# GpSimd turns both heads of the second pair, and the stacking transfers are issued one slot earlier

## The chip, the cores and the metric

The kernel runs on one core of one Trainium2 chip. The metric is the device time of one execution in microseconds (us); lower is better. A core has five engines that run side by side, each through its own instructions in order: TensorE (PE in the rows; its weight loads are PEld), VectorE (DVE), ScalarE (ACT), GpSimd (POOL) and SyncE (SP), which here issues every transfer by DMA. Engines wait for each other and for transfers by semaphores.

## The reference, cut to what matters

Attention with rotary position embedding, and behind it two feed-forward blocks. The change lies in the attention.

```python
B, H, S, D = 4, 8, 576, 64                     # q, k, v
rotate(x) = concat([x1 * cos - x2 * sin, x1 * sin + x2 * cos])   # x1, x2: halves of D
scores = rotate(q) @ rotate(k).T / sqrt(D)
attn = exp(scores - max); attn = attn / (sum(attn) + 1e-9)
x = attn @ v                                   # then as (2304, 512)
x = (sigmoid(x @ w_gate) * (x @ w_val)) @ w_out            # 512 -> 1536 -> 512
h = x @ w_in; solu = h * softmax(h); out = layernorm(solu) * g_ln @ w_out2
```

## The kernel before, in words

The 32 pairs of batch and head are worked on two heads at a time: 16 pairs (`pairs`, numbered 0 to 15 here). A pair has nine tiles of 128 queries, and the main loop goes through 16 x 9 = 144 slots, one tile of queries in each. In a slot TensorE makes the scores (`scores`, tile `s`, line 364), VectorE takes the negative maximum (`row_max`, `nm`, line 371), ScalarE the exponentials with their sums (`exps`, `e`, line 376); TensorE transposes `e` (`te`), and ScalarE and VectorE take it out of PSUM as a high and a low part (`et`, lines 426 and 429, `evac_h` and `evac_l`); TensorE multiplies by v (`av`, line 476). Every matrix product is made of high and low parts, so that operands are kept twice.

Work that belongs to other pairs is woven into the slots by a table, `SLOTS`: a number there is a slot counted from the first slot of the pair that it is for. `at(...)` puts a call into the agenda of a slot, and within a slot calls stand in the order in which they were put there, the lower pair first. For pair i:

- `load_qk` brings q and k (`raw`, lines 208 and 212), `load_v` brings v (`rawv`, lines 220 and 225).
- `turn` rotates q and k of both heads in four steps, two products (line 242) and two sums (line 250), on GpSimd unless it is told another engine. For pair 1 it was called for head 0 on GpSimd and for head 1 on VectorE. Pair 0 is turned by `turn_first` (lines 266 and 250).
- `qk_bank` transposes the result on TensorE (`tq`, lines 298 and 301), and it is taken out of PSUM into the tile `st` (lines 426 and 429), at slots -11, -9 and -8.
- `stack` lets five transfers by SP copy halves of `st` between the partitions (lines 310 to 314), since scores need high and low parts above each other. The fourth and fifth write over what the first three read, so SP stands at line 313 until those have landed. Behind all five come the first `scores` of the pair. Pairs 0 and 1 are stacked by ScalarE and VectorE as well (`stack_first`, lines 323 to 329).
- `split_v` (ACT line 281, POOL line 282) splits v; `stack_left` (line 335) copies the last 64 queries to the tile `qtl`.
- After the pair's scores: `weigh` adds 1e-9 to the sums on GpSimd (line 388) and takes the reciprocal on VectorE (line 389); `weigh_out` stores it to DRAM (`d<-rt`, line 403); `spread` reads it back to all partitions in four transfers (`wt<-d`, line 411); `join` moves one head's output beside the other's (`um<-uw`, line 482), `add` adds the two parts on GpSimd (line 488), and `scale_x` multiplies by the weights on GpSimd (line 421).

SP, GpSimd and VectorE go through this strictly in order, so what a table entry moves is also a place in three queues. In slot 21 of pair i-3 stands its `spread`, which is the slot -6 of pair i.

Of the kernel before, what the change touches and what calls it, by code (L numbers as in the profile page):

```python
# [20 lines left out]
def kernel(  # L21
# [21 lines left out]
    nc = tc.nc  # L43
# [158 lines left out]
    def load_qk(i, t=None):  # L202

        b, hp = pairs[i]
        hs = slice(2 * hp, 2 * hp + 2)
        raws[i] = t = raw_p.tile([P, 2, NSL, D], F32, tag="raw", name=f"raw{i}") if t is None else t
        for j, src in enumerate((k, q)):
            yield nc.sync.dma_start(
                out=t[:, :, 4 * j:4 * j + 4, :], in_=src[b, hs, 0:MAIN, :].rearrange("h (p r) d -> p h r d", r=4)
            )  # L210
        for j, src in enumerate((k, q)):
            yield nc.sync.dma_start(
                out=t[j * LEFT:(j + 1) * LEFT, :, 8, :], in_=src[b, hs, MAIN:S, :].rearrange("h t d -> t h d")
            )

    def load_v(i):
        b, hp = pairs[i]
        hs = slice(2 * hp, 2 * hp + 2)
        t = rawv_p.tile([P, 10, D], F32, tag="rawv", name=f"rawv{i}")
        nc.sync.dma_start(  # L220
            out=t[:, 0:8, :].rearrange("p (h r) d -> p h r d", h=2),
            in_=v[b, hs, 0:MAIN, :].rearrange("h (p r) d -> p h r d", r=4),
        )
        for j in range(2):
            nc.sync.dma_start(
                out=t[j * LEFT:(j + 1) * LEFT, 8:10, :], in_=v[b, hs, MAIN:S, :].rearrange("h t d -> t h d")
            )
        vraws[i] = t
# [3 lines left out]
    def turn(i, step, hs=slice(0, 2), eng=nc.gpsimd):  # L232

        if i not in others:
            others[i] = rot_p.tile([P, 2, NSL, D], F32, tag="other", name=f"other{i}")
        if step == 2 and i not in turned:
            turned[i] = rot_p.tile([P, NSL, 2, D], F32, tag="turned", name=f"turned{i}")
        n = NSL * (hs.stop - hs.start)
        x, o = (t[:, hs].rearrange("p h i (a d) -> p (h i) a d", a=2) for t in (raws[i], others[i]))
        if step < 2:  # L240
            w = rope_sb[:, 1 - step, hs].rearrange("p h i d -> p (h i) d").unsqueeze(2)
            eng.tensor_mul(out=(o, x)[step], in0=x, in1=w.to_broadcast([P, n, 2, D // 2]))
        else:
            turn_end(i, step, eng, hs, slice(0, NSL))

    def turn_end(i, step, eng, hs, sl):
        a = step - 2
        here, there = (slice(c * D // 2, (c + 1) * D // 2) for c in (a, 1 - a))
        op = eng.tensor_sub if a == 0 else eng.tensor_add
        op(  # L250
            out=turned[i][:, sl, hs, here].rearrange("p i h d -> p h i d"),
            in0=raws[i][:, hs, sl, here],
            in1=others[i][:, hs, sl, there],
        )

    def turn_first(table):

        others[0] = rot_p.tile([P, 2, NSL, D], F32, tag="other", name="other0")
        turned[0] = rot_p.tile([P, NSL, 2, D], F32, tag="turned", name="turned0")
        x, o = (t.rearrange("p h i (a d) -> p h i a d", a=2) for t in (raws[0], others[0]))  # L260
        for hs, sl, eng in FIRST_PARTS:
            n = sl.stop - sl.start
            for step in range(2):
                for h in range(hs.start, hs.stop):
                    w = rope_sb[:, 1 - step, h, sl] if sl.start == 4 else table[:, 1 - step, sl if n > 1 else slice(4, 5)]
                    eng.tensor_mul(
                        out=(o, x)[step][:, h, sl], in0=x[:, h, sl],
                        in1=w.unsqueeze(2).to_broadcast([P, n, 2, D // 2]),
                    )
            for step in (2, 3):  # L270
                turn_end(0, step, eng, hs, sl)
# [16 lines left out]
    def qk_bank(i, part):  # L288

        raw = turned[i].rearrange("p i h d -> p i (h d)")  # L290
        if part == 0:
            stacks[i, 0] = qk_p.tile([P, 2, 2, S], F32R, tag="st0", name=f"st0_{i}")
            stacks[i, 1] = qk_p.tile([P, 3, S], F32R, tag="st1", name=f"st1_{i}")
        st = stacks[i, 0]
        ps = ps_t.tile([P, 512], F32, tag="t", name=f"tq{i}_{part}")
        if part < 2:
            for r in range(4):
                nc.tensor.transpose(ps[:, r * P:(r + 1) * P], raw[:, 4 * part + r, :], ident)
            h_out, l_out, src = st[:, 0, part, 0:MAIN], st[:, 1, part, 0:MAIN], ps
        else:  # L300
            nc.tensor.transpose(ps[:, 0:P], raw[:, 8, :], ident)
            h_out, l_out = st[:, 0, :, MAIN:S], st[:, 1, :, MAIN:S]
            src = ps[:, 0:P].rearrange("p (a t) -> p a t", a=2)
        return [(h_out, l_out, src)]
# [215 lines left out]
    FIRST, GROUP, ATTEND, REST = "first", "group", "attend", "rest"  # L520
    agenda = {}

    def at(g, kind, fn, *args):
        agenda.setdefault((g, kind), []).append((fn, args))


    SLOTS = dict(
        te=(1, 3, 4, 5, 6, 7, 8, 9, 11),
        corner=8,
        left=(6, 11),  # L530
        av=(((6, 2), (8, 9)), ((9, 4), (10, 9)), ((11, 2), (12, 6), (13, 9)), ((14, 9),)),
        join=(18, 19),
        add=(20, 24),
        weigh=11,
        weigh_t=13,
# [2 lines left out]
        scale=24,  # L538
        turn=(-16, -16, -15, -15),
        bank=(-11, -9, -8),  # L540
        stack=-6,
        split_v=-1,
        stack_left=0,
        load_qk=-23,
# [6 lines left out]
        bank1=(1, 1, 1),  # L551
        stack1=3,
        first_b=(-1, -1, 2),
        turn1=(0, 0, 0, 0),
        split_v0=0,
        stack_left0=0,
    )
# [60 lines left out]
    def evacuate_h(evs):  # L618
        for ev in evs:
            evac_h(*ev)  # L620
# [58 lines left out]
    if True:  # L679

        spare_1 = et_p.tile([P, 16 * S], F32, tag="et", name="spare1")
        table = spare_1[:, 2 * NSL * D:2 * NSL * D + 2 * 5 * D // 2].rearrange("p (c i d) -> p c i d", c=2, i=5)
        first_loads = load_qk(0)
        next(first_loads)
        nc.sync.dma_start(out=table, in_=rope)
        for _ in first_loads:
            pass
        for h in range(2):
            nc.scalar.activation(out=rope_sb[:, :, h, 4:8], in_=table[:, :, 0:4], func=AF.Copy, scale=D ** -0.5)
        for _ in load_qk(1, spare_1[:, 0:2 * NSL * D].rearrange("p (h i d) -> p h i d", h=2, i=NSL)):  # L690
            pass
        nc.sync.dma_start(out=g_sb, in_=moe2_g_ln.rearrange("(k p) -> p k", p=P))
        load_v(0)
        load_v(1)
        turn_first(table)
        for h in range(2):
            nc.scalar.copy(out=rope_sb[:, :, h, 0:4], in_=table[:, :, 0:4])
            nc.scalar.copy(out=rope_sb[:, :, h, 8:9], in_=table[:, :, 4:5])
        first.extend(qk_bank(0, part)[0][2] for part in range(3))
        for m in range(3):  # L700
            stack_first(0, m)
            at(SLOTS["first_b"][m], REST, stack_first, 1, m)
        at(SLOTS["stack_left0"], REST, stack_left, 0)
        at(SLOTS["split_v0"], REST, split_v, 0)
        for m in range(4):
            turn(1, m, slice(0, 1))
            at(SLOTS["turn1"][m], REST, turn, 1, m, slice(1, 2), nc.vector)
        for fn, args in agenda.pop((-1, REST), []):
            fn(*args)

        sc = scores(0, 0)
        for g in range(NPR * NTL):
            i, n = divmod(g, NTL)
            if g == (NPR - 1) * NTL:
                prep_ctx.close()
                xs_pool["p"] = x_ctx.enter_context(tc.tile_pool(name="xs", bufs=XS, side="right", reuse_waits="tile"))
            if g == 1:
                et = et_p.tile([P, 2, 2, 4, S], F32R, tag="et", name="et")
            nm = row_max(i, n, sc)
            if SLOTS["exp_pos"] == 0:  # L720
                exps(i, n, sc, nm)
            evacuate_h(cur)
            if SLOTS["exp_pos"] == 1:
                exps(i, n, sc, nm)
            evacuate_h(late)
            if SLOTS["exp_pos"] == 2:
                exps(i, n, sc, nm)
            evacuate_u()
            if SLOTS["exp_pos"] == 3:
                exps(i, n, sc, nm)  # L730
            evacuate_l()
            if g + 1 < NPR * NTL:
                sc = scores(*divmod(g + 1, NTL))
            advance(g)
# [381 lines left out]
```

## Time and profile before

| | |
|---|---|
| median of 3 runs | 980.09 us (976.26 to 981.96) |
| the profiled execution, its own time | 977.19 us |
| its span, from first to last instruction | 975.4 us |
| PE, DVE, ACT, POOL busy in the span | 933.8, 651.7, 505.5, 445.6 us |
| transfers issued by SP, share of 16 DMA engines | 34.6% |
| attention, first score to last | 11.5 to 299.3 us |
| granted TensorE clock, mean | 0.998 of full speed |

Busy shares over the whole span mix three stages. The attention ends near 300 us, and only there do the changed lines run; after it comes the first feed-forward block and then the second.

### The profile page before, as it was taken

How to read it: one execution, taken by the hardware profiler on the slowest of the kernel's cores; microseconds unless marked ns; L12 is line 12 of the kernel's file. 1: busy time of each engine (PE TensorE's matmuls, PEld its weight loads, DVE VectorE, ACT ScalarE, POOL GpSimd, SP SyncE). 2: the span in 40 equal slices, each digit the busy share in tenths (PEclk: the TensorE clock that was granted, in tenths of full speed). 3: DMA queues.
4: the chain of work that ended last, by engine and by line, in shares of the span. 5: the costliest groups of instructions: out<-in, count | busy, mean ns of one | idle time of the engine just before them, and what ended most of it. 6: DMA issues, size and time to landing. Idle time of an engine off the chain costs nothing.

```text
span 975.4 us, 14436 instructions
## 1 busy us (share of the span) xinstructions
PE 933.8 (96%) x5128; PEld 798.6 (82%) x5128; DVE 651.7 (67%) x1073; ACT 505.5 (52%) x994; POOL 445.6 (46%) x356
## 2 busy tenths in 40 slices
PE   4999999999999899999999999999999989999998
PEld 3889899898988588898788898788898868888886
DVE  8999989999988945346245365544456787666561
ACT  4889989898986323133111123112123576666662
POOL 5668889889835533334314344324343531121110
PEclk9999999999999999999999999999999999999999
DMA  4666677676654320103101012100111334334231
GB/s 109 142 163 165 156 184 180 162 177 154 166 131 133 90 65 22 44 23 100 30 22 42 24 44 87 44 22 22 44 45 63 109 64 88 66 75 87 65 76 44
DMA packets 92311, 86.10 MB, mean 88 GB/s; under 512 B 52608, under 2 KB 77456, under 8 KB 92240
## 3 DMA queue, kind: packets, MB, share of 16 engines
q1 hardware_dynamic: 92240, 85.19, 34.6%
q8 instruction: 40, 0.66, 0.3%
q14 instruction: 31, 0.25, 0.1%
HBM read 46.83 MB, written 4.79 MB: 53 GB/s over the span
## 4 chain that ended last, share of the span: by engine, by line
PE 63%; DVE 13%; DMA 10%; POOL 6%; issue 4%; SPq 2%; ACT 2%; DVEq 0%; POOLq 0%; ACTq 0%
PE gv L673 9%; PE gv L674 9%; PE gv L672 9%; DMA st<-st 8%; PE y L783 4%; PE y L782 4%; PE y L781 4%; PE po L970 3%; PE po L969 3%; PE po L971 3%; PE ph L874 3%; PE ph L876 3%; PE ph L875 3%; DVE nm L371 2%; DVE val L121 2%
## 5 line engine op out<-in xcount | busy, mean ns | idle before, releaser
L767 POOL TENSOR_TENSOR gs<-g,gs 128x512 fp32r<-128x512 f32 (+1 forms) x59 | 74.1, 1256 | 268.1 <-DVE gs L766 242.0
L762 ACT ACTIVATE sg<-gv 128x512 f32<-128x512 f32 (+1 forms) x60 | 33.3, 556 | 295.9 <-PE gv L674 295.9
L672 PE MATMUL gv<-xs,w 128*128 128x512 f32 (+1 forms) x480 | 178.5, 372 | 2.3 <-ACT w L135 2.3
L674 PE MATMUL gv<-xs,w 128*128 128x512 f32 (+1 forms) x480 | 178.6, 372 | 2.1 <-POOL w L136 1.7
L673 PE MATMUL gv<-xs,w 128*128 128x512 f32 (+1 forms) x480 | 178.6, 372 | 0.3 <-DVE xs L507 0.2
L764 DVE TENSOR_TENSOR g<-gv,sg 128x512 f32<-128x512 f32 (+1 forms) x60 | 38.2, 636 | 181.4 <-ACT sg L762 181.3
L364 PE MATMUL s<-st 128*128 128x288 f32 x512 | 103.1, 320 | 15.3 <-DMA st<-st 8.1
L376 ACT ACTIVATE e<-s,nm 128x576 f32<-128x576 f32 x144 | 107.8, 748 | 19.0 <-DVE nm L371 17.7
L371 DVE TENSOR_REDUCE nm<-s 128x1 f32<-128x576 f32 x144 | 107.3, 746 | 5.5 <-PE s L364 4.0
L674 PEld LDWEIGHTS gv<-xs,w 128*128 128x128 f32 x480 | 90.0, 188 | 20.8 <-POOL w L136 2.8
L672 PEld LDWEIGHTS gv<-xs,w 128*128 128x128 f32 x480 | 90.0, 188 | 20.2 <-ACT w L135 3.2
L673 PEld LDWEIGHTS gv<-xs,w 128*128 128x128 f32 x480 | 90.1, 188 | 18.9 <-DVE xs L507 1.9
L429 DVE TENSOR_TENSOR et<-te,et 128x512 fp32r<-128x512 f32 x144 | 98.7, 687 | 10.1 <-ACT et L426 8.2
L476 PE MATMUL av<-et,vs 128*128 128x288 f32 x512 | 99.5, 315 | 0.7 <-DVE uw L625 0.5
L364 PEld LDWEIGHTS s<-st 128*128 128x128 f32 x512 | 75.3, 193 | 25.3 <-ACT e L376 9.0
L783 PE MATMUL y<-gs,w 128*128 128x512 f32 (+1 forms) x240 | 89.3, 372 | 0.0
L781 PE MATMUL y<-gs,w 128*128 128x512 f32 (+1 forms) x240 | 89.1, 371 | 0.0
L782 PE MATMUL y<-gs,w 128*128 128x512 f32 (+1 forms) x240 | 89.1, 371 | 0.0
L435 PE MATMUL te<-ident,e 128*128 128x128 f32 x576 | 86.4, 273 | 0.3 <-DVE et L429 0.3
L426 ACT CAST et<-te 128x512 fp32r<-128x512 f32 x144 | 84.1, 586 | 3.0 <-PE te L435 2.8
L476 PEld LDWEIGHTS av<-et,vs 128*128 128x128 f32 x512 | 72.9, 189 | 2.2 <-DVE uw L625 1.6
L435 PEld LDWEIGHTS te<-ident,e 128*128 128x128 f32 x576 | 70.8, 141 | 0.7 <-DVE et L429 0.5
(128 smaller groups left out, 1963.8 us busy)
## 6 DMA issues: line engine op xcount, KB each, us to landing
wraw<-in_moe_w_out_dram SPq DMA_DIRECT2D x20, 512.0 KB, 3.9
st<-st SPq DMA_DIRECT2D x30, 288.0 KB, 3.1
st<-st SPq DMA_DIRECT2D x15, 432.0 KB, 4.0
wraw<-in_moe_w_gate_dram SPq DMA_DIRECT2D x12, 512.0 KB, 4.1
wraw<-in_moe_w_val_dram SPq DMA_DIRECT2D x12, 512.0 KB, 4.8
um<-uw SPq DMA_DIRECT2D x32, 144.0 KB, 2.4
st<-st SPq DMA_DIRECT2D x30, 144.0 KB, 4.9
rawv<-in_v_dram SPq DMA_DIRECT2D x16, 256.0 KB
```

Source lines behind the costliest of these rows:

```text
L364: nc.tensor.matmul(ps[:, j, :HALF], w, x, start=m == 0, stop=m == len(mm) - 1)
L371: nc.vector.tensor_reduce(out=nm, in_=ps[:, :, :HALF], axis=AX.XY, op=ALU.max, negate=True)
L376: nc.scalar.activation(out=e.rearrange("p (j c) -> p j c", j=2), in_=ps[:, :, :HALF], func=AF.Exp, bias=nm, accum_out=sums[i][:, sum_at[n] ...
L429: nc.vector.tensor_sub(out=l_out, in0=ps, in1=h_out.bitcast(F32))
L435: nc.tensor.transpose(ps[:, r * P:(r + 1) * P], e[:, r * P:(r + 1) * P], ident)
L476: nc.tensor.matmul(av[:, :HALF], *mm[m], start=m == 0, stop=m == len(mm) - 1)
L672: nc.tensor.matmul(ps[:, :n], wh, x[:, 0, :n], start=kk == 0, stop=False)
L673: nc.tensor.matmul(ps[:, :n], wh, x[:, 1, :n], start=False, stop=False)
L674: nc.tensor.matmul(ps[:, :n], wl, x[:, 0, :n], start=False, stop=kk == KD - 1)
L781: nc.tensor.matmul(ys[m][:, :n], wh, g[:, 0, :n], start=first, stop=False)
L782: nc.tensor.matmul(ys[m][:, :n], wl, g[:, 0, :n], start=False, stop=False)
L783: nc.tensor.matmul(ys[m][:, :n], wh, g[:, 1, :n], start=False, stop=last)
```

## The change

Two things change. The entry `stack` of the table goes from -6 to -7, so that the five stacking transfers of pairs 2 to 15 are put into the agenda one slot earlier. And for pair 1 `turn` is called once for both heads on GpSimd, where it was called for head 0 on GpSimd and for head 1 on VectorE.

```diff
@@ SLOTS
         bank=(-11, -9, -8),
-        stack=-6,
+        stack=-7,
         split_v=-1,
...
-        turn1=(0, 0, 0, 0),
@@ before the main loop
         for m in range(4):
-            turn(1, m, slice(0, 1))
-            at(SLOTS["turn1"][m], REST, turn, 1, m, slice(1, 2), nc.vector)
+            turn(1, m)
```

On SP, the rows from the stacking of pair 4 to that of pair 5 stood like this before (`st_4` and `st_5` are the pairs' tiles, `wt` is the spread of pair 1 and then 2, `raw` the loads of pair 6).

```order
L310 DMA st_4_946<-st_4_945 64x1728
L311 DMA st_4_946<-st_4_945 64x1152
L312 DMA st_4_946<-st_4_945 64x576
L313 DMA st_4_945<-st_4_945 64x1152
L314 DMA st_4_945<-st_4_945 64x576
L208 DMA raw_1141<-in_k_dram 128x2x256
...
L482 DMA um_1290<-uw_0_919 64x576
L482 DMA um_1290<-uw_1_1067 64x576
L220 DMA rawv_1320<-in_v_dram 128x2x256
L225 DMA rawv_1320<-in_v_dram 64x2x64 x2
L411 DMA wt_1384<-d_1175 64x512 x2
L411 DMA wt_1384<-d_1175 64x64 x2
L310 DMA st_5_1224<-st_5_1223 64x1728
```

With the change they stand like this.

```order
L314 DMA st_4_941<-st_4_941 64x576
L411 DMA wt_1108<-d_895 64x512 x2
L411 DMA wt_1108<-d_895 64x64 x2
L208 DMA raw_1137<-in_k_dram 128x2x256
...
L403 DMA d_1171<-rt_1169 9x128
L482 DMA um_1286<-uw_0_915 64x576
L482 DMA um_1286<-uw_1_1063 64x576
L220 DMA rawv_1316<-in_v_dram 128x2x256
L225 DMA rawv_1316<-in_v_dram 64x2x64 x2
L310 DMA st_5_1220<-st_5_1219 64x1728
```

The four `wt` transfers of a spread went from just ahead of a pair's five stacking transfers to just behind them; nothing else changed its place on SP, and the same happens at pairs 4 to 15.

On GpSimd, the start of the program differs in the rows that turn pair 1 (`spare_131` holds its q and k, `turned_206` the result).

```order
-L242 TENSOR_TENSOR other_203<-spare_131,rope_sb 128x576
-L242 TENSOR_TENSOR spare_131<-spare_131,rope_sb 128x576
-L250 TENSOR_TENSOR turned_206<-spare_131,other_203 128x9x32 x2
+L242 TENSOR_TENSOR other_203<-spare_131,rope_sb 128x1152
+L242 TENSOR_TENSOR spare_131<-spare_131,rope_sb 128x1152
+L250 TENSOR_TENSOR turned_206<-spare_131,other_203 128x2x9x32 x2
 L335 CAST qtl_78<-st_0_179 128x64
 L335 CAST qtl_78<-st_0_180 128x64
 L282 TENSOR_TENSOR vs_239<-rawv_145,vs_239 128x10x64
```

The same four instructions are twice as wide, and the copies to `qtl`, the split of v and the turn of pair 2 follow behind them as before. On VectorE, at the same time, four instructions are gone between the maxima of the first two tiles of queries.

```order
 L371 TENSOR_REDUCE nm_0_223<-s_0_217 128x1
-L242 TENSOR_TENSOR other_203<-spare_131,rope_sb 128x576
-L242 TENSOR_TENSOR spare_131<-spare_131,rope_sb 128x576
-L250 TENSOR_TENSOR turned_206<-spare_131,other_203 128x9x32 x2
```

The maximum of the second tile now follows that of the first directly. On TensorE and ScalarE no instruction changes its place.

## Rows read from the trace of the kernel before

**Rows 1.** Busy time by stretch, one pair each: engines, granted clock, DMA share, GB/s.
```profile
103.31:121.60 18.29, 16.80 (x132) 16.11 (x132) 17.20 (x30) 16.88 (x41) 14.63 (x11) 1.00 0.64 154
...
211.29:229.31 18.02, 16.72 (x132) 16.19 (x132) 17.75 (x29) 15.57 (x37) 15.80 (x12) 1.00 0.70 170
```

**Rows 2.** Waits, 60 to 290 us: us in total, times, longest us.
```profile
PE s L364 <- DMA st<-st: 7.8, 15, 1.2
```

**Rows 3.** Timeline of TensorE at the end of pair 5: start, us, what, idle before.
```profile
119.12 0.63 PE L298 MATMUL tq<-ident,turned 128*128 128x128 f32 x4
120.89 0.37 PE L364 MATMUL s<-st 128*128 128x288 f32 x1 [1.14 <-DMA st<-st]
121.60 0.67 PE L364 MATMUL s<-st 128*128 128x288 f32 x3 [0.34 <-DMA st<-st]
```

**Rows 4.** Timeline of SP's issues between the stackings of pairs 5 and 6.
```profile
99.96 0.54 SPq L314 DMA_DIRECT2D st<-st  x1
...
104.14 1.15 SPq L482 DMA_DIRECT2D um<-uw  x2
...
107.39 2.47 SPq L411 DMA_DIRECT2D wt<-d  x4
110.35 0.48 SPq L310 DMA_DIRECT2D st<-st  x1
```

**Rows 5.** Timeline of VectorE at the same place.
```profile
110.04 0.28 DVE L429 TENSOR_TENSOR st<-tq,st 128x128 fp32r<-128x128 f32 x1
110.24 0.21 DVE L389 RECIPROCAL sum<-sum 128x9 f32<-128x9 f32 x1
```

**Rows 6.** Timeline of SP at the stacking of pair 9.
```profile
165.31 0.54 SPq L310 DMA_DIRECT2D st<-st  x1
```

**Rows 7.** Timeline of VectorE at the stacking of pair 9.
```profile
164.44 0.28 DVE L429 TENSOR_TENSOR st<-tq,st 128x128 fp32r<-128x128 f32 x1
```

**Rows 8.** Timeline of GpSimd in pair 5.
```profile
101.19 1.42 POOL L421 TENSOR_TENSOR x_sb<-x_sb,wt 128x576 f32<-128x576 f32 x1
105.01 1.57 POOL L282 TENSOR_TENSOR vs<-rawv,vs 128x640 fp32r<-128x640 f32 x1 [2.40 <-ACT vs L281]
...
106.90 1.45 POOL L488 TENSOR_TENSOR x_sb<-uw,um 64x576 f32<-64x576 f32 x1
108.43 0.25 POOL L388 TENSOR_SCALAR sum<-sum 128x9 f32<-128x9 f32 x1
...
114.28 2.82 POOL L250 TENSOR_TENSOR turned<-raw,other 128x576 f32<-128x576 f32 x2
```

**Rows 9.** Transfers, 60 to 280 us: count, KB each, median us to landing.
```profile
um<-uw SPq DMA_DIRECT2D x24, 144.0 KB, 2.4
...
wt<-d SPq DMA_DIRECT2D x24, 16.0 KB, 2.9
```

**Rows 10.** Timeline of GpSimd at the start.
```profile
10.02 1.40 POOL L242 TENSOR_TENSOR other<-spare,rope_sb 128x576 f32<-128x576 f32 x1 [1.51 <-DVE turned L250]
11.50 1.41 POOL L242 TENSOR_TENSOR spare<-spare,rope_sb 128x576 f32<-128x576 f32 x1
...
22.27 2.64 POOL L242 TENSOR_TENSOR raw<-raw,rope_sb 128x1152 f32<-128x1152 f32 x1
```

**Rows 11.** Timeline of VectorE at the start.
```profile
11.73 1.50 DVE L329 CAST st<-st 64x576 fp32r<-64x576 f32 x1
...
15.66 0.76 DVE L242 TENSOR_TENSOR other<-spare,rope_sb 128x576 f32<-128x576 f32 x1
...
17.25 2.17 DVE L250 TENSOR_TENSOR turned<-spare,other 128x288 f32<-128x288 f32 x2
...
23.08 2.15 DVE L329 CAST st<-st 64x576 fp32r<-64x576 f32 x1
```

**Rows 12.** Timeline of TensorE at the start.
```profile
19.57 1.94 PE L298 MATMUL tq<-ident,turned 128*128 128x128 f32 x8 [1.69 <-DVE turned L250]
...
25.37 0.90 PE L364 MATMUL s<-st,qtl 128*128 128x288 f32 x5 [1.15 <-DVE st L329]
```

## The prediction, made before the changed kernel was run

> **What bounds the kernel now.** I first read the busy time by stretch, cut at the starts of pairs, because the change lies in the attention alone and a share over the whole span says nothing there. The reader sees that TensorE and VectorE are both nearly full: in the stretch of pair 5 TensorE is busy 16.80 us and VectorE 17.20 us of 18.29 us, and in pair 11 VectorE is busy 17.75 us of 18.02 us [rows 1]. So an idle microsecond of VectorE may or may not be covered, depending on the pair. Next I read the waits: TensorE waits 7.8 us in 15 waits for the stacking transfers `st<-st`, all at the first scores of a pair [rows 2]; the worst case is the end of pair 5, where it stands 1.14 us and then 0.34 us, 1.48 us together [rows 3]. That is what an earlier stacking could win. Then I asked what starts the stacking. The transfer of line 310 is issued at 110.35 us. VectorE finishes the last part of `st` at 110.04 + 0.28 = 110.32 us, and SP had finished the spread ahead of it at 107.39 + 2.47 = 109.86 us [rows 4, 5]. The stacking is released by VectorE's data, not by its place in SP's queue.
>
> **The change, part by part. The order on SP.** Between two stackings SP issues the same transfers as before; only the spread goes from their end to their beginning. So SP is free for the next stacking at the same time as before, and the data come when they came: the first scores gain nothing in a pair like that of rows 4. There are pairs in which SP was late: in pair 9 the data are there at 164.44 + 0.28 = 164.72 us and line 310 is issued at 165.31 us, 0.59 us later [rows 6, 7]. There the spread, now early, fills time in which SP waited for `uw` and `rt`, and part of the 0.59 us may come back. I take 0.5 us for the whole run, between 0 and 1.0 us.
>
> **What is now late.** Everything that SP issues between the stackings comes 2.47 us later, and the spread itself much later. GpSimd stands behind both. In pair 5 the stacking's last issue ends at 99.96 + 0.54 = 100.50 us [rows 4]. The spread would be issued from 100.55 us; its last transfer starts some 1.9 us on (three quarters of 2.47) and lands 2.9 us after that [rows 4, 9], at 105.35 us. `scale_x`, which ran at 101.19 us, waits for it, and ends at 105.35 + 1.42 = 106.8 us; `split_v` and the two copies to `qtl` behind it take 106.90 - 105.01 = 1.89 us, to 108.7 us [rows 8]. The other way gives the same: `um` is issued at 104.14 + 2.47 = 106.61 us and lands 2.4 us later, at 109.0 us [rows 4, 9]. So the first `add` begins near 109.05 us, not 106.90 us, 2.15 us late, and the sum of line 388, which ends 108.43 + 0.25 - 106.90 = 1.78 us after the add began, is ready at 110.83 us [rows 8]. VectorE reaches the reciprocal that needs it at 110.24 us [rows 5]. It must stand 0.6 us, and queued behind it are the maximum and the `et` parts of the next tiles, for which ScalarE and TensorE wait. The stacking is not hit: its data are written just ahead of the reciprocal.
>
> **How much of that reaches the end.** Where TensorE waits for the stacking at the end of the pair, 0.6 us of delay disappears in that wait (1.48 us in pair 5). The sum of these waits, 7.8 us over the twelve pairs concerned, is 0.65 us for each, as large as the stall, but uneven: pair 11, with 0.27 us of VectorE's time free, has no cover. I take two pairs of nine or ten that lose their 0.6 us: 1.2 us, between 0 and 9 x 0.6 = 5.4 us.
>
> **The turn.** GpSimd's turn in pair 5 ends at 114.28 + 2.82 = 117.10 us, and `tq` starts at 119.12 us [rows 8, 3]. 2.15 us later it ends at 119.25 us, so `tq` starts up to 0.15 us late. Right behind `tq` stands the wait of 1.48 us that hides it; I take nothing. Without that cover it would be 0.15 us a pair, 1.8 us in twelve.
>
> **Pair 1.** VectorE loses the four instructions from 15.66 us to 17.25 + 2.17 = 19.42 us, and `tq` of pair 1 starts behind them at 19.57 us [rows 11, 12]. GpSimd starts its turn at 10.02 us [rows 10]. At full width a product takes 2.64 us and, as between the two at half width (11.50 - 10.02 - 1.40), 0.08 us pass before the next, 2.72 us from start to start [rows 10]; the two sums take 2.82 us [rows 8]: 10.02 + 2 x 2.72 + 2.82 = 18.3 us, 1.1 us ahead of VectorE's end. The next thing on VectorE is the cast of line 329. In both rows it lasts until 0.32 us after the GpSimd product beside it: 11.73 + 1.50 = 13.23 us against 11.50 + 1.41 = 12.91 us, and 23.08 + 2.15 = 25.23 us against 22.27 + 2.64 = 24.91 us [rows 10, 11]. With the change GpSimd begins pair 2's turn at 18.3 us, plus 1.89 us for the copies and the split [rows 8], plus 0.2 us of gaps: 20.4 us. Its first product ends near 23.1 us, the cast comes near 22.0 us and ends at 23.4 us instead of 25.23 us. TensorE waits for that cast (1.15 us at 25.37 us, [rows 12]), and from there on runs without a long pause. The gain is between 1.1 us (`tq`) and 1.8 us (cast); I take 1.6 us. If the cast is more than 1 us later than I think it falls into the second product and ends after 23.1 + 2.72 + 0.32 = 26.1 us, 0.9 us late. So the bounds are a gain of 1.8 us and a loss of 0.9 us. Pair 2's turn then ends near 20.4 + 2 x 2.72 + 2.82 = 28.7 us, and its transposes are called only in slot 7 of pair 0.
>
> A product that VectorE did in 0.76 us takes GpSimd 1.40 us at the same size [rows 10, 11], a factor of 1.84, so the move makes work; it gains only because GpSimd begins 5.6 us earlier. The Trainium skill (GPSIMD Engine Reference, "Engine selection") speaks against such a move: two-input elementwise work is about twice as slow on GpSimd. An estimate by that factor gives a product of both heads 4 x 0.76 = 3.04 us and, with the sums as long as a product, an end at 10.02 + 3 x 3.04 = 19.1 us; the gain at `tq` would be 0.3 us, not 1.1 us. The rows have the durations themselves, so they decide.
>
> **The sum.** -0.5 - 1.6 + 1.2 = -0.9 us on the profiled execution's 977.19 us (span 975.4 us and 1.8 us around it), which gives 976.3 us. That execution lies 2.9 us below the median of the runs, 980.09 us; on the median it is 979.2 us. What a measurement here can tell from no change is about 0.5%, 4.9 us.
>
> **The rivals.** *The stacking lands earlier* (faster). If freeing the transfers from the spread ahead of them, in SP's queue or in the DMA engines, ended TensorE's waits, all 7.8 us would go: 980.1 - 7.8 - 1.6 = 970.7 us. For it speaks that the spread is issued 0.5 us ahead of line 310; against it, that line 310 waited for VectorE until 110.32 us. *The late sum stops VectorE in every pair* (slower). The place is the reciprocal; it decides from the point where the sum comes more than a pair's cover late, 1.48 us in pair 5 and less elsewhere. If the spread or `um` landed 1 us later than before, nine stalls of 1.6 us less the cover of 7.8 us leave 6.6 us, together with the other terms +4.5 us: 984.6 us. For it speaks that both ways into the add are late at once; against it, that 0.6 us is within most covers. *The first cast loses to GpSimd* (little change). With wide products the cast that came at 11.73 us could wait for the second one, to 10.02 + 2 x 2.72 + 0.2 = 15.7 us instead of 13.23 us. VectorE's next pieces shift by 2.4 us, the third scores end near 20.3 us, and `tq` behind them is 0.7 us later than before instead of earlier: +0.7 - 0.5 + 1.2 = +1.4 us, 981.5 us. Against it: in both rows the cast got in after one product. The Trainium skill (SBUF — State Buffer, "Who interferes with whom") has the rule behind this rival: a cast of VectorE in a two-port mode and a GpSimd instruction exclude each other for the whole instruction, and the one that issues first goes first. The 0.32 us in both rows agree with it; who goes first beside wider products no row shows.
>
> **How the numbers follow.** My forecast 0.62, the earlier stacking 0.10, the stop in every pair 0.16, the lost cast 0.12. The range takes the bounds of the terms (-2.8 us at best without the rival, +7.2 us at worst) with the median's own spread in three runs, and reaches half way to the first rival: 973.5 to 985.0 us. Faster by over 0.5%: the first rival and little else, 0.14. Slower by over 0.5%: the worse half of the second and a tail, 0.13. Within 0.5%: 0.73.
>
> **What would show it.** Right: line 310 still starts within 0.1 us of VectorE's last part of `st`; `scale_x` and the first add wait for `wt` and `um`; the reciprocal is preceded by an idle 0.5 to 0.7 us that ends with GpSimd's sum; TensorE's waits for `st<-st` shrink by about what VectorE lost; pair 1's `tq` starts near 18.4 us and the second cast ends near 23.4 us. Wrong: pairs that last over 0.5 us longer with the wait at the reciprocal over 1 us, or pairs of 17.1 us without waits for `st<-st`.

## The result, and the profile of the changed kernel

The changed kernel takes 987.95 us (median of 6 runs, 985.64 to 992.3), the kernel before on the same chip 975.92 us (6 runs, 974.93 to 981.96). The ratio is 1.0108, with a 95% interval from 1.0085 to 1.013: slower by 1.1%, above my range. The profiled execution took 985.64 us, its span is 983.9 us.

Of the two parts of the change, the turn of pair 1 came as worked out. The timelines of GpSimd, VectorE and TensorE at the start answer to [rows 10 to 12]:

```profile
10.05 2.62 POOL L242 TENSOR_TENSOR other<-spare,rope_sb 128x1152 f32<-128x1152 f32 x1 [1.51 <-DVE turned L250]
...
15.57 2.77 POOL L250 TENSOR_TENSOR turned<-spare,other 128x576 f32<-128x576 f32 x2
...
20.18 2.67 POOL L242 TENSOR_TENSOR other<-raw,rope_sb 128x1152 f32<-128x1152 f32 x1
```

```profile
11.75 1.24 DVE L329 CAST st<-st 64x576 fp32r<-64x576 f32 x1
...
21.94 1.22 DVE L329 CAST st<-st 64x576 fp32r<-64x576 f32 x1
```

```profile
18.40 1.97 PE L298 MATMUL tq<-ident,turned 128*128 128x128 f32 x8 [0.77 <-POOL turned L250]
...
23.31 0.91 PE L364 MATMUL s<-st,qtl 128*128 128x288 f32 x5 [0.48 <-DVE st L329]
```

GpSimd's turn ends at 18.34 us, `tq` starts at 18.40 us (I said 18.4), and the second cast ends at 23.16 us (I said 23.4). Pair 5 starts at 101.20 us, not 103.31 us [rows 1]: 2.1 us gained, where I had taken 1.6 us.

All of that and more is then lost. I cut the attention from the second score product of pair 4 to that of pair 15, eleven pairs. Three views of busy time by stretch follow (columns as in [rows 1]): the eleven pairs of the changed kernel, those of the kernel before, and pairs 5 and 11 of the changed kernel.

```profile
84.10:290.10 206.00, 187.94 (x1437) 176.90 (x1437) 187.59 (x306) 176.04 (x413) 158.81 (x120) 1.00 0.65 158
```

```profile
86.20:281.80 195.60, 185.71 (x1437) 176.99 (x1437) 182.07 (x306) 176.20 (x412) 160.03 (x120) 1.00 0.69 165
```

```profile
101.20:119.86 18.66, 17.26 (x132) 16.13 (x131) 17.33 (x30) 17.14 (x42) 14.65 (x12) 1.00 0.64 153
...
213.90:235.53 21.63, 17.28 (x131) 16.26 (x132) 19.14 (x29) 15.45 (x37) 17.14 (x13) 1.00 0.62 156
```

Eleven pairs last 10.4 us longer. VectorE is busy 5.52 us longer with the same number of instructions (x306), so some of its instructions have become slower; and pair 11 alone lost 3.61 us (21.63 against 18.02 us), 1.39 us of it in VectorE's busy time. The clock was full in both, so it isn't that. The waits from 60 to 290 us, first of the changed kernel, then of the kernel before (the stacking's is in [rows 2]):

```profile
ACT e L376 <- DVE nm L371: 19.8, 23, 2.1
...
PE s L364 <- ACT e L376: 9.9, 12, 1.7
...
DVE sum L389 <- POOL sum L388: 7.1, 7, 2.4
POOL x_sb L488 <- DMA um<-uw: 6.1, 6, 2.2
...
PE s L364 <- DMA st<-st: 4.1, 8, 1.2
```

```profile
ACT e L376 <- DVE nm L371: 8.1, 18, 1.5
...
PE s L364 <- ACT e L376: 1.7, 3, 0.7
...
DVE sum L389 <- POOL sum L388: 1.1, 1, 1.1
```

VectorE waits 7.1 us at the reciprocal (before 1.1 us, once), and TensorE now waits 9.9 us for exponentials that stand behind VectorE (before 1.7 us), while its wait for the stacking fell from 7.8 to 4.1 us. What stood there, in pair 11, on GpSimd, SP and VectorE:

```profile
217.51 1.57 POOL L282 TENSOR_TENSOR vs<-rawv,vs 128x640 fp32r<-128x640 f32 x1
...
221.32 1.44 POOL L488 TENSOR_TENSOR x_sb<-uw,um 64x576 f32<-64x576 f32 x1 [1.89 <-DMA um<-uw]
222.85 0.25 POOL L388 TENSOR_SCALAR sum<-sum 128x9 f32<-128x9 f32 x1
...
225.89 2.65 POOL L242 TENSOR_TENSOR raw<-raw,rope_sb 128x1152 f32<-128x1152 f32 x1
```

```profile
211.19 2.81 SPq L411 DMA_DIRECT2D wt<-d  x4
...
217.49 1.15 SPq L482 DMA_DIRECT2D um<-uw  x2
```

```profile
220.64 0.28 DVE L429 TENSOR_TENSOR st<-tq,st 128x128 fp32r<-128x128 f32 x1
223.13 0.21 DVE L389 RECIPROCAL sum<-sum 128x9 f32<-128x9 f32 x1 [2.22 <-POOL sum L388]
...
226.72 2.38 DVE L121 SCALAR_TENSOR_TENSOR val<-mag,val 128x512 int32<-128x512 int32 x1
```

The reader sees two things. First, `um` is issued behind the moved spread, the add starts 3.83 us after that issue, and VectorE stands 2.22 us for the sum. GpSimd stood idle for the last 1.89 us of that, so `um` itself took long as well. The profile tells the landing of only a few `um` transfers: in the changed kernel from 60 to 290 us, and in the kernel before from 60 to 280 us:

```profile
DMA to landing us min/median/max: 2.4/2.7/4.5
```

```profile
DMA to landing us min/median/max: 2.3/2.4/4.6
```

A landing as slow as that was there before the change as well. In the DMA records of 215 to 224 us two packets of instructions lie beside the data (`um` is 144 KB; the columns are packets, MB, share of 16 engines):

```profile
q8 instruction: 1, 0.02, 1.1%
q14 instruction: 1, 0.01, 0.5%
```

That such a packet made `um` late is argued from the time, not shown: the slowest landing of the first view, of a transfer issued at 198.10 us, has no packet of instructions beside it, but a 512 KB weight load issued just ahead of it (197.43 us). Second, line 121 takes 2.38 us. It is one of VectorE's shifts with two inputs in SBUF that decode feed-forward weights, woven into pairs 7, 9 and 11, and it ends (229.10 us) 0.56 us after GpSimd's product of line 242 (228.54 us), which began 0.83 us ahead of it. All three executions of each of the two shifting lines, in the view of one source line, changed kernel first:

```profile
L121 DVE SCALAR_TENSOR_TENSOR val<-mag,val x3: 2375/2404/2412, 149.9 to 226.7; 128x512 int32<-128x512 int32 x3
...
L124 DVE SCALAR_TENSOR_TENSOR val<-wraw,val x3: 681/1714/1723, 155.0 to 231.8; 128x512 int32<-128x512 int32 x3
```

```profile
L121 DVE SCALAR_TENSOR_TENSOR val<-mag,val x3: 679/1042/1819, 150.5 to 221.8; 128x512 int32<-128x512 int32 x3
...
L124 DVE SCALAR_TENSOR_TENSOR val<-wraw,val x3: 681/681/1740, 153.9 to 225.6; 128x512 int32<-128x512 int32 x3
```

Line 121 grows by 7.19 - 3.54 = 3.65 us and line 124 by 4.12 - 3.10 = 1.02 us: 4.7 us of the 5.52 us. The Trainium skill (SBUF — State Buffer, "Who interferes with whom") says that a VectorE instruction with two SBUF inputs and a GpSimd instruction that reads SBUF exclude each other, whichever issues first. The rows agree: the shift ends 0.56 us after the product, and alone it takes 0.68 us.

### The profile page after: what moved, and what is told of

Same layout as the page of the kernel before. It is cut to its first block, busy times and chain, and to the rows that moved or that the text cites. A ratio compares the mean times of both kernels' runs of the same rounds, so it can differ in the third digit from the quotient of the medians.

```text
span 983.9 us, 14406 instructions
## 1 busy us (share of the span) xinstructions
PE 936.5 (95%) x5128; PEld 799.7 (81%) x5128; DVE 652.0 (66%) x1069; ACT 505.5 (51%) x994; POOL 447.8 (46%) x356
## 4 chain that ended last, share of the span: by engine, by line
PE 63%; DVE 14%; DMA 10%; issue 4%; POOL 4%; SPq 2%; ACT 2%; POOLq 0%; DVEq 0%; ACTq 0%
PE gv L672 9%; PE gv L673 9%; PE gv L671 9%; DMA st<-st 8%; PE y L781 4%; PE y L779 4%; PE y L780 4%; PE po L968 3%; PE po L967 3%; PE po L969 3%; PE ph L872 3%; PE ph L873 3%; PE ph L874 3%; DVE nm L371 3%; DVE et L429 2%
```

## The experiments

**Theories.** A: the late spread makes GpSimd late, by `um` and `wt`, and VectorE waits at the reciprocal. B (rival): GpSimd's new timing puts its products over VectorE's shifts. C (rival): the stacking's new place on SP is itself the harm. Ratios are to the kernel before on the same chip. "Eleven pairs" is the stretch from the second score of pair 4 to that of pair 15 in the profiled execution: before 195.6, changed 206.0 us. It is one execution of each kernel, so it can differ from the medians by some us.

**The two halves of the change.**

```diff
 e1_stack_only, on the kernel before:   -stack=-6  +stack=-7
 e2_turn_only, on the changed kernel:   -stack=-7  +stack=-6
```

> The table entry of the stacking at -7, pair 1 turned by both engines as before. If the loss is all the spread's new place on SP (theory A), the gain at the start is missing and the loss stays: the pairs from 5 on lose the 10.4 us that the changed kernel's trace shows, 985 to 990 us, ratio to before 1.010 to 1.014. If the loss came with the turn on GpSimd (theory B), this one is as fast as before, 975 to 978 us.

> Pair 1 turned on GpSimd alone, the stacking at -6 as before. Theory A: about 2 us faster than before (first scores of pair 4 near 84.1 us instead of 86.2 us), 973 to 975 us, ratio 0.997 to 0.9985, and the pairs behind keep their length. Theory B: slower than before by most of the 10 us.

Stacking alone: 1.0118 (1.0102 to 1.0133); turn alone: 0.9968 (0.9955 to 0.998), 974.75 us against 978.06 us. The whole loss is the table entry, and the turn alone gains 2.0 to 4.4 us, as the 2.1 us of the trace; its eleven pairs take 195.6 us. Line 121 took 1.67 to 2.41 us in the first and 0.68 to 1.79 us in the second.

**The sum on VectorE.** This takes the reciprocal away from GpSimd's queue.

```diff
-        sum_eng=0,
+        sum_eng=1,
```

> The changed kernel with the 1e-9 added to the sums by VectorE, so that its reciprocal no longer waits for GpSimd. If the wait at the reciprocal (7.1 us in 7 pairs) is the whole loss, the time comes down to that of the turn alone, 973 to 976 us. If VectorE's weight decoding under GpSimd's turn is the larger part, only some 3 to 5 us come back: 982 to 985 us, and line 121 still takes about 2.4 us in its three pairs.

1.0142 (1.0128 to 1.0156), eleven pairs 209.9 us: slower still, a miss. The wait is gone, and line 121 took only 0.87 to 1.15 us in pairs 7, 9 and 11, but the addition of nine numbers a partition now runs on VectorE beside GpSimd's product. One such place, on VectorE and on GpSimd:

```profile
92.98 2.77 DVE L388 TENSOR_SCALAR sum<-sum 128x9 f32<-128x9 f32 x1
95.78 0.21 DVE L389 RECIPROCAL sum<-sum 128x9 f32<-128x9 f32 x1
```

```profile
93.05 2.66 POOL L242 TENSOR_TENSOR other<-raw,rope_sb 128x1152 f32<-128x1152 f32 x1
```

It ends at 95.75 us, 0.04 us after the product, though it is recorded 0.07 us ahead of it, at the end of an add of GpSimd; so the recorded starts don't tell who goes first here. Over twelve pairs it took 0.17 to 2.77 us. It speaks for B's kind of harm, and shows that the remedy for A runs into it at a new place.

**Decoding two to four slots later.**

```diff
-        decode=(3, 5, 13, 15, 23, 29),
+        decode=(3, 5, 17, 18, 23, 29),
```

> The changed kernel with VectorE's two shifting steps of the decoding called at slots 17 and 18 of their units, where GpSimd waits for the spread, not 13 and 15. If the port shared with GpSimd holds them, lines 121 and 124 take about 0.7 us each and 4 to 5 us come back: 982 to 984 us, with the waits at the reciprocal still there. If these durations don't matter to the end, 986 to 989 us as the changed kernel.

1.0099 (1.0076 to 1.0122), eleven pairs 203.9 us. Line 124 now took 1.40 to 1.83 us at its new place, line 121 0.68 to 1.55 us. Together the six shifts fell from 11.3 to 7.8 us (before 6.6 us), but the eleven pairs by 2.1 us only. It neither proves nor refutes B.

**No sum on GpSimd.** The 1e-9 of line 388 is left out.

```diff
-        (nc.gpsimd, nc.vector)[SLOTS["sum_eng"]].tensor_scalar_add(sm, sm, 1e-9)
```

> The changed kernel with the addition of 1e-9 to the sums left out, so that VectorE's reciprocal waits for nothing on GpSimd (the sums are over 1, so 1e-9 is below their precision). If the wait at the reciprocal is the whole loss, 973 to 977 us, ratio to the kernel before about 0.998. If it is a part beside VectorE's decoding held by GpSimd's turn, about half comes back: 980 to 984 us.

1.0055 (1.0029 to 1.0081), eleven pairs 201.3 us. Without any wait at the reciprocal over half the loss against the turn alone stays; line 121 took 1.88 to 2.59 us. A alone isn't enough.

**Which late input.** Three kernels place `spread`, `scale` and `join` of pairs differently; `stack` stays at -7.

```diff
 e6_scale_late:         scale of pairs 0 to 12: slot 24 -> 31    (only um is late)
 e7_spread_behind_um:   spread, scale of pairs 1 to 12: slots 21, 24 -> 28, 31   (nothing is late)
 e8_um_ahead:           join: slots (18, 19) -> (12, 19)    (first um right behind the spread, ahead of the loads)
```

> The changed kernel with the scaling by the spread weights called at slot 31, behind the turn, for pairs 0 to 12: the spread no longer holds GpSimd, only the 2.47 us by which SP issues the um transfers later is left. If um's delay alone is enough to make the sum late, the waits at the reciprocal stay and the time is 984 to 990 us. If it was the spread that held GpSimd, 974 to 978 us.

> The changed kernel with the spread of pairs 1 to 12 called at slot 28, so that on SP it stands behind the first um transfer, and the scaling at slot 31. The stacking stays at -7, and neither um nor the spread is late for GpSimd. If the lateness of these two is the cause, the time is that of the turn alone, 972 to 977 us, with no wait at the reciprocal. If the stacking's earlier place itself costs, 984 to 990 us.

> The changed kernel with the first um transfer called at slot 12 and not 18, so that SP issues it right behind the spread and ahead of the loads: um is no longer late, and only the spread holds GpSimd. If the spread alone is enough, the sum stays late by some 2 us and the time is 984 to 989 us. If um was what made it late, 974 to 978 us.

1.0098 (1.0076 to 1.012), 0.9979 (0.9961 to 0.9997) and 1.0067 (1.0042 to 1.0091). With the spread behind `um` the new place of the stacking costs nothing: C falls. The later `scale`, which this kernel has too, didn't do it: alone it left 1.0098. The waits at the reciprocal from 60 to 290 us, in this order:

```profile
DVE sum L389 <- POOL sum L388: 5.6, 7, 2.1
```

```profile
DVE sum L389 <- POOL sum L388: 0.5, 1, 0.5
```

```profile
DVE sum L389 <- POOL sum L388: 1.2, 6, 0.3
```

So `um` makes the sum late; with `um` early, line 121 still took 2.42 us each time, and 1.0% over the turn alone stays (1.0067 against 0.9968). With the spread behind `um` line 121 takes 0.68 to 0.72 us; line 124 takes 1.74 to 1.89 us there, and still nothing is lost (eleven pairs 195.7 us), so a longer shift doesn't cost at every place.

**No shifts.** Lines 121 and 124 are left out for the three pieces of weights that are decoded inside the attention, so these are not decoded; one kernel also leaves out the 1e-9. The base is the turn alone without shifts.

```diff
 e9_no_shifts, e10_no_shifts_no_add, e11_turn_only_no_shifts, lines 121 and 124:
-        )
+        ) if i else None
```

> The changed kernel with the two shifting steps of the decoding (lines 121 and 124) left out for the three units decoded inside the attention, so that their weights are wrong and VectorE has six instructions less. What stays is the wait at the reciprocal. If decoding under GpSimd's turn is half of the loss, 980 to 983 us; if it is beside the point, 985 to 988 us less the six instructions' own 0.7 us each where VectorE is the bound.

> The changed kernel without the two shifting steps and without the addition of 1e-9: neither mechanism is left. If the two are the whole loss, the same time as the turn alone without the shifting steps, within 1.5 us, near 972 to 976 us. A third mechanism would leave it slower than that by its share.

> The base for the two runs before it: the turn on GpSimd alone, stacking at -6, without the two shifting steps of the three units. 971 to 975 us, that is 0 to 3 us under the turn alone, since the shifting steps took 0.7 to 1.8 us each there and most of it was covered by waits for the stacking.

1.0031 (1.0013 to 1.005), 1.0025 (1.0006 to 1.0044), 0.9949 (0.9931 to 0.9967). The eleven pairs, in the order base, without shifts, without shifts and sum, and without the sum alone (the kernel of **No sum on GpSimd**):

```profile
83.75:278.88 195.13, 184.65 (x1438) 176.98 (x1438) 177.18 (x300) 175.83 (x413) 157.86 (x120) 1.00 0.68 166
```

```profile
83.64:283.40 199.76, 186.85 (x1438) 176.85 (x1438) 178.48 (x300) 175.81 (x413) 156.27 (x120) 1.00 0.67 163
```

```profile
89.14:288.45 199.31, 186.19 (x1438) 178.20 (x1438) 178.07 (x301) 176.55 (x413) 152.98 (x109) 0.99 0.67 164
```

```profile
83.81:285.11 201.30, 186.79 (x1437) 176.70 (x1438) 187.90 (x306) 177.09 (x413) 155.45 (x109) 1.00 0.66 161
```

Of the 10.4 us that the changed kernel lost, 199.8 - 195.1 = 4.7 us stay without the shifts and 201.3 - 195.6 = 5.7 us without the sum, so either alone takes away about half. But they don't add up: with both away 199.3 - 195.1 = 4.2 us stay in the eleven pairs, and in the repeat below 200.8 - 195.1 = 5.7 us. The medians say the same: of 1.0108 - 0.9968 = 1.4%, with both away 1.0025 - 0.9949 = 0.76% stays. A and B are parts of the loss, and about half of it stays without them.

**The turn alone, decoding later.** `e2_turn_only` with decoding in slots 16 and 16, not 13 and 15.

> The turn on GpSimd alone with both shifting steps called at slot 16, when GpSimd adds and scales in pieces of 1.4 us and not turns in pieces of 2.7 us, and TensorE is about to wait for the stacking. If the port holds them less there, 1 to 2 us under the turn alone, 972 to 974 us; if VectorE's backlog reaches the stacking's data, as it did with slots 17 and 18, 976 to 979 us.

1.0 (0.9984 to 1.0015): no gain, slower than the turn alone. The six shifts took 6.4 us, not less than there (6.3 us), and the eleven pairs 198.7 us: no better place was found for them in the old order.

**What stays without A and B.** The kernel without shifts and sum again, with `um` ahead (`join` in slot 12), and with the first transposes one slot later (`bank` -10, not -11).

> The changed kernel without the decoding shifts and without the add of 1e-9, once more, because the profiled execution of the first look had a lower granted clock in pairs 1 to 4. If what it lost against the turn alone without shifts (about 4 us from pair 4 to pair 15, 0.76% by ratio) is the moved spread's own, it is there again: ratio to before 1.0025 within 0.002, and TensorE waits again about 4 us at the transposes of line 298 for GpSimd's turn. If it was the disturbed execution, the trace shows pairs of 17.1 to 18.1 us as with the turn alone, and no such wait.

> The same, with the calls that move one head's output (um) put six slots earlier, so that of GpSimd's three inputs only the spread is late. If the remainder is the late turn at TensorE's transposes, and the turn is late because GpSimd waits for um, the 4.4 us of waits at line 298 go and the ratio falls to that of the turn alone without shifts, 0.995. If GpSimd is late by the spread itself, the waits stay and the ratio is about 1.002.

> The same as the first, with the first of a pair's three transposes one slot later (slot -10, not -11), and nothing else. If the remainder is TensorE standing at line 298 for the turn, these waits go and the ratio falls towards 0.995 to 0.998. If the remainder is in the waits for the stacking (st), it stays at 1.002 or grows, since st is taken out of PSUM no earlier than before.

1.0022 (0.9994 to 1.005), 1.0029 (1.0009 to 1.0048), 1.0048 (1.0021 to 1.0076). It stays, with `um` ahead too. In the repeat TensorE waits like this from 60 to 290 us:

```profile
PE s L364 <- DMA st<-st: 7.9, 13, 1.6
PE tq L298 <- POOL turned L250: 3.3, 3, 1.8
```

The wait at the transposes for GpSimd's turn is not the remainder by itself: with later transposes it is gone, and the kernel is no faster. The clock shows a part of it. TensorE's timeline in the repeat at the start of pair 2, and its busy time by stretch there; then the same at the start of pair 11:

```profile
48.32 0.37 PE L364 MATMUL s<-st 128*128 128x288 f32 x1 [0.21 <-DMA st<-st]
50.34 0.66 PE L364 MATMUL s<-st 128*128 128x288 f32 x3 [1.65 <-DMA st<-st]
```

```profile
50.30:51.00 0.70, 0.66 (x5) 0.66 (x6) 0.00 (x0) 0.12 (x1) 0.51 (x1) 0.94 0.33 77
51.00:54.30 3.30, 3.30 (x17) 3.28 (x15) 1.53 (x3) 1.12 (x3) 3.30 (x4) 0.50 0.14 50
```

```profile
215.95 0.37 PE L364 MATMUL s<-st 128*128 128x288 f32 x1 [1.65 <-DMA st<-st]
```

```profile
215.90:222.00 6.10, 5.75 (x44) 5.57 (x45) 4.39 (x8) 4.14 (x12) 3.17 (x4) 1.00 0.66 187
```

At pair 2 TensorE waits 1.65 us for the stacking, and from 51.0 to 54.3 us its granted clock is 0.50 of full speed, 1.2 instead of 2.4 GHz; TensorE is busy all that time, so by my estimate 3.3 us at half speed cost 1.65 us more. At pair 11 a wait of the same length is followed by full clock, so the length of one wait doesn't decide it. This execution has four such spells from 20 to 340 us, the first execution of the same kernel four, the turn alone without shifts, and the kernel before, none. Four of about 1.7 us are 6.8 us, the size of the 0.7%; that is an estimate from one execution, and the fourth spell, at 331 us, lies behind the attention, where the turn alone too has one (320 to 327 us).

In the kernel with `um` ahead eleven pairs take 195.9 us, as in the turn alone; in that execution the loss is behind them. It is the fastest of ten (977.62 us, median 981.39 us), so a part of what the median lost doesn't stand in this profile. TensorE in pair 15 of that kernel, then SP's issues at that place in the changed kernel, where the same happens in small:

```profile
289.04 1.33 PE L364 MATMUL s<-st 128*128 128x288 f32 x4 [3.65 <-ACT e L376]
```

```profile
287.35 2.81 SPq L411 DMA_DIRECT2D wt<-d  x4
290.20 0.51 SPq L403 DMA_DIRECT2D d<-rt  x1
290.75 0.37 SPq L104 DMA_DIRECT2D wraw<-in_moe_w_gate_dram  x1
```

```profile
297.30:302.00 4.70, 4.70 (x25) 4.67 (x26) 3.19 (x7) 3.63 (x9) 1.68 (x2) 0.64 0.07 13
```

Two feed-forward weight loads stand in slot -4 of pair 15, now directly behind the spread. ScalarE and VectorE wait for them (1.48 and 1.33 us in the changed kernel), TensorE stands 1.93 us, and the clock is 0.64 over the next 4.70 us (the last row, of the changed kernel).

**The weight loads early**, in the changed kernel, without shifts and sum, and with `um` ahead as well.

```diff
-        at((NPR - 1) * NTL - 4, REST, w_load, *x)
+        at((NPR - 1) * NTL - 8, REST, w_load, *x)
```

> The changed kernel with two feed-forward weight loads (line 104, for pair 15) issued four slots earlier, ahead of the moved spread and not behind it. Theory: behind the spread they land late, ScalarE (line 119) and VectorE (line 120) stand 1.5 us for them, TensorE stands 1.93 us at line 364 and its granted clock falls to half from 297 to 302 us; without that some 1.5 to 3.5 us come back, ratio 1.0075 to 1.009, and the granted clock stays at 1.0 there. If TensorE's pause there has another cause (the sum, line 388), the clock still falls and the ratio stays at 1.011.

> The same early weight loads in the kernel without the decoding shifts and without the add of 1e-9 (1.0022 and 1.0025 before). If the remainder is the late weight loads, the ratio falls to 0.995 to 0.998. If it is TensorE standing at the transposes and the stacking in pairs 1 to 14, with its clock falling behind the longest of these waits, the ratio falls by 0.1 to 0.3% only, and the clock is below 1 in some pair again.

> All four repairs: no decoding shifts, no add, um six slots earlier and the weight loads early. The profiled execution of the kernel without the last of these lost nothing in pairs 4 to 15 (195.9 us against 195.1 us of the turn alone) and some 4 us behind pair 15's second score. If the list of causes is complete, the ratio is that of the turn alone without shifts, 0.995 within 0.002; if something is missing, it stays at 1.0 or above.

1.0089 (1.0069 to 1.0109), 1.0011 (0.9992 to 1.0029), 0.9989 (0.997 to 1.0007). In the first the clock stays full around 297 us, but falls at 333 us instead, and its eleven pairs take 205.9 us (changed kernel 206.0 us). The first two are not told apart from the kernels without the early loads: the intervals overlap. The third is, narrowly: 1.0029 with `um` ahead alone, 0.9989 with the early loads as well, and the intervals don't meet; TensorE's wait in pair 15 is 1.85 us in that profile and not 3.65 us, and the clock behind it is full. The list isn't complete: 0.4% stays against 0.9949. In the last profile two waits of pair starts are followed by half clock, at 69 and 124 us.

## Why the prediction was wrong

- **The order on SP, right.** In pair 6 line 310 is issued at 108.50 us, VectorE's last part of `st` ends at 108.47 us, and SP was free at 107.55 us. The earlier entry gained nothing, and with the spread behind `um` it cost nothing either.
- **Pair 1, right,** 2.1 us instead of 1.6 us; the lost cast did not happen: the first cast again ended 0.32 us after the first product (12.99 and 12.67 us).
- **What is now late, right in kind.** In the pair where I worked it out the wait was 0.27 us, I had said 0.6 us. But I let `um` land 2.4 us after its issue, the median, in every pair, where the trace before has landings up to 4.6 us. In pair 11 the add started 3.83 us after the issue, in pair 13 `um` landed 4.28 us after it, and VectorE waited 2.22 and 2.43 us. Those two make 4.65 of the 7.1 us.
- **"How much of that reaches the end", the step that failed.** I took 1.2 us, between 0 and 5.4 us; the eleven pairs lost 10.4 us. My term, the wait at the reciprocal, was mis-sized: 7.1 us in seven waits, where I counted 0.6 us in each of two pairs. Without it 4.7 us of the 10.4 us come back. And the shifts are in no term: I asked who waits for GpSimd, and not what runs beside it. GpSimd's 2 us put its products on VectorE's shifts, which took 4.7 us longer in six instructions; without them 5.7 us come back. I had used that rule for the cast of pair 1, and not for the pairs in which the table decodes weights.
- **The cover, wrong.** I let the stall disappear in TensorE's waits for the stacking. They shrank by 7.8 - 4.1 = 3.7 us, as predicted in kind. But with A and B away they are 7.9 us again in the repeat, and 3.3 us for the turn come to them. So what is taken from VectorE's stops partly returns as waits of TensorE, which fits that taking away A and B together gave little more than either; that these waits are all of the rest is not shown.
- **The turn, taken as nothing because a wait would hide it:** line 298 waited 3.7 us in four waits for GpSimd's add that stands behind the turn and 0.6 us in two for the turn itself, before 2.5 us in four and nothing: 1.8 us more at most, which was my upper bound. With A and B away TensorE waited 3.3 us in three waits for the turn.
- **The range.** It didn't follow from its terms: the worst case of +7.2 us on the median of 980.09 us is 987.3 us, and the range ended at 985.0 us. Pair 1's 0.9 us, the 5.4 us and the turn's 1.8 us add up to 8.1 us, not 7.2 us. The measured difference of the medians, 987.95 - 975.92 = 12.0 us, lies above that too; and the median before had been 980.09 us in three runs and came to 975.92 us in six.
- **The rival** "stops VectorE in every pair" (984.6 us) came nearest, for a part of the reason: VectorE stopped in seven of twelve pairs, and the shifts were not in it.

Open: why the stacking lands late in some pairs of the kernels with the moved spread. Pair 2 of the repeat has no spread beside it; an instruction packet lies in the window of its stacking, but no run took that packet away. Why the clock falls after some of these waits and not after others is open too. Of the last 0.4% no run shows the cause; these waits, and the clock behind some of them, are all that the profiles show.

The best version is the turn alone, 0.9968 (974.75 us); with the spread behind `um` and the entry at -7 it is 0.9979 (0.9961 to 0.9997), not told apart from it.

## What to carry to other kernels

When an entry of a queue moves, list not only who waits for the engine that becomes late, but also what each of its long instructions will now lie beside: here a delay of 2 us cost about as much by overlap as by waiting. Price a wait by the slow landings in the trace too, not by the median alone, and follow every transfer that the moved one passes to the end of the stage, as the weight loads of pair 15. And when two causes are taken away and half of the loss stays, don't share the loss out between them; look where the waits went, and read the granted clock by stretch before looking for a third wait.

## What the hardware showed that I had not expected

- An addition of nine numbers a partition took VectorE 2.77 us beside a GpSimd product, and 0.17 us at its shortest.
- A wait of TensorE of 1.65 us was followed by 3.3 us at 1.2 GHz, so by the estimate above it cost twice its length; another of 1.65 us and one of 1.82 us in the same execution were followed by full clock. One of 3.65 us was followed by a granted clock of 0.57 over the next 7.0 us. The two profiled executions of the same kernel without shifts and sum had one fall at the same place (51 us) and three at different ones, and in the kernel before a wait of 1.14 us was followed by none [rows 3].
